# Three decoding passes for float64 weights instead of four, and a new set of ranks, in a downsampled-plus-local attention and gated MLP kernel

## The chip, the cores and the metric

One core of a Trainium2 chip runs the whole program. The metric is device microseconds of one launch. Three runs of the kernel before gave 586.04, 587.34 and 1143.34 us, median 587.34 us.

## The reference

For 8 batches and 8 heads of 576 positions by 64 dimensions, two attentions are added. The first averages q, k and v over groups of 4 positions, takes softmax attention over the 144 groups and repeats each result 4 times. The second is attention within a band: position i sees j only where |i - j| < 4.

```
pos = np.arange(S)
mask = np.abs(pos[:, None] - pos[None, :]) < factor
...
return (out_up + out_local).astype(np.float32)
```

The sum, with heads side by side, is x of shape (8, 576, 512). A gated MLP follows:

```
h = np.maximum(x @ w_in, 0.0)
u, v = (h[..., :d_ff // 2], h[..., d_ff // 2:])
v_n = (v - mu) / np.sqrt(var + 1e-06)
v_s = np.einsum('ts,bsd->btd', w_spatial, v_n) + b_spatial[None, :, None]
return ((u * v_s) @ w_out).astype(np.float32)
```

w_in (512 x 1024) and w_out (512 x 512) arrive as float64, which no engine of the kernel computes in: their 32-bit halves are read as integers and made into float32 on the chip.

## The kernel before

The work is a list of pieces. A piece is one instruction or a short group on one engine, with the buffers that it reads and writes, a planned duration and a rank. `Plan.run` walks the pieces as a list scheduler does: on each engine it takes, of the pieces that can start within NEAR ns of the first one that can, the one of lowest rank. What it emits is a fixed order for each engine; each engine then runs its instructions strictly in that order and waits at each for what it needs. The ranks stand in tables (RANK for attention, MRANK for the MLP, WRANK for the weights) and the strings in ON say, for the n-th piece of a kind, which engine or which variant it takes (A ScalarE, D VectorE, P GpSimd; for "mask", T adds the mask by a matmul and D on VectorE).

Names, used below as in the profile:

- Attention works on 32 pairs of heads (n = 0 to 31, four to a batch). S is the banded score matmul (L751 lays the mask down, L758 the scores), T transposes the probabilities (L854), AV multiplies by v (L962). Sd, Td, AVd are the same for the averaged attention (L820, L901, L929). With "sub" on A the maximum only becomes a bias (L790) and ScalarE does ten activations of 64 columns (L798); on D VectorE subtracts (two instructions, L786) and ScalarE does one activation of 640 columns (L801). "sum" (L730, L733) averages q and k; "normd" (L883 on ScalarE, L886 elsewhere) scales the averaged attention's probabilities. The result x of a pair is written as a high half on ScalarE (xa to xg, L1012) and a low half on VectorE (L1014), and its last 64 positions are copied to xtail (L1016).
- MLP, per batch: V are five matmul pieces (four of L1039, one tail L1044), evicted by L1057; U are eight (L1102, evicted by L1105); SP are eight (L1134, gated on L1155), O four (L1170) and one tail piece for two batches (L1185).
- Weights: w_in's V half (WV), its U half (WU), w_spatial (WSP) and w_out (WO). WV, WU and WO come in four pieces of 128 x 512 float64 each. A piece is fetched (L523) into stg or more, decoded into one of six buffers mba to mbf, summed up in absolute value on ScalarE (L658) for a scale, and split into a float16 high half on ScalarE (L511) and a low half on VectorE (L514). V of a batch needs all of WV and x of the batch's four pairs; U needs all of WU; SP all of WSP.
- The four decoding passes, per piece, are d1 (multiply the upper word, read as float32, by 2^-112; ScalarE L541, or VectorE or GpSimd L543), d2 (shift left by 3 and clear the sign, VectorE L546), d3 (fetch the sign from the product and join it, VectorE L550) and d4 (join the top three bits of the lower word, VectorE L555). GpSimd and VectorE pieces that the program holds to share a port carry `port=True` and are never planned at the same time; d4 does not carry it.
- Where the plan sees TensorE idle in the first 110 us it puts in filler matmuls on constants (L1214) that compute nothing.

In the order that results, the first 80 us hold the loads, the decoding and the attention of the first pairs, and the rest is the steady part in which the MLP of one batch is interleaved with the attention of the next.

Of the kernel before, what the change touches and what calls it, by code (L numbers as in the profile page):

```python
# [8 lines left out]
F32 = mybir.dt.float32  # L9
# [3 lines left out]
I32 = mybir.dt.int32  # L13
# [63 lines left out]
class Plan:  # L77
# [61 lines left out]
    def run(self, near=150.0, stay=0.0, dma=(1900.0, 900.0), emit=True):  # L139
# [17 lines left out]
        while left:  # L157
# [95 lines left out]
RANK = {"load": [90.169, 257.539, 303.907, -159.662, -510.639, -25.642, 405.455, -297.525, 5.13, 264.367, 351.699, 276.06,  # L253
            682.221, 54.868],
        "vload": [434.68, 234.812, 262.794, 74.315, 728.463, -15.228, -243.297, -31.858],
        "vabs": [467.345, -1170.291, -136.803, -260.041, -345.091, 133.278, -941.516, 12.316],
        "tv": [-84.809, 64.704, 479.328, 995.501, 350.344, -198.277, -346.695, -222.775],
        "sum": [-132.552, -211.417, -218.297, -329.655, 364.902, 111.471, 91.479, 393.607, 1763.478, 137.899, -76.822, 739.926,
            -40.013, 64.573],
        "S": [-671.111, -532.057, 271.346, -585.398, -841.898, 478.333, 18.826, -602.428, 177.33, 40.497, 208.693, 271.364,  # L260
            160.961, 247.816],
        "E": [-754.564, -306.398, -710.714, 213.708, 122.695, 238.643, 42.123, 1057.27, -571.18, -741.81, -241.921, -309.788,
            -379.446, -245.978],
        "N": [351.195, -536.694, -589.965, 590.836, -96.063, 629.51, 1122.526, -174.004, 0.365, -36.852, -359.038, -336.375,
            646.961, -94.987],
        "T": [-226.254, -238.971, -1086.855, -450.305, 760.115, -1472.718, -853.117, 276.295, 490.91, -182.776, -192.183,
            -37.547, -339.778, 39.198],
        "Sd": [85.837, -47.061, -984.686, -195.937, -159.211, -44.271, -280.964, 516.618, 1316.646, -337.627, -261.865, 184.375,
            -269.138, -135.441],
        "Nd": [271.663, -564.046, -555.506, -129.335, -1202.018, -327.324, -477.611, -101.539, -269.892, 119.203, 541.338, 147.5,  # L270
            341.705, 491.194],
        "Td": [-63.802, 166.781, 912.991, 171.397, -207.967, -74.563, 1024.918, -842.706, -306.265, 29.991, -143.29, -121.336,
            -992.41, -238.063],
        "AVd": [239.818, -835.613, -260.738, 73.129, 507.866, 908.357, 67.434, -40.584, -197.477, 92.972, -337.272, -1.96,
            -132.091, 143.162],
        "AV": [190.318, -438.664, -462.749, 692.051, -804.089, 72.948, 440.132, -392.904, -551.022, 39.946, -326.512, -51.248,
            5.793, -319.964],
        "X": [134.737, -356.693, 84.463, -85.637, -382.379, 453.739, 25.853, 353.509, 251.441, 230.484, -271.172, 149.233,
            -52.957, -25.463]}
MRANK = {"V": [[16.513, 67.783], [-623.639, -792.169], [-416.323, 106.304], [-263.565, -49.834], [-261.378, 39.119], [-352.403,  # L280
            38.031], [-368.389, 30.748], [-34.568, -55.986]],
        "U0": [[-275.497, 276.444], [50.68, -65.887], [170.332, 454.518], [262.672, -77.469], [-62.913, 15.29], [51.586,
# [977 lines left out]
```

## Time and profile before

| | |
|---|---|
| median of three runs | 587.34 us |
| the profiled execution | 586.45 us |
| its span, first to last instruction | 584.7 us |
| around the span | 1.75 us |
| TensorE busy | 557.9 us (95%) |
| VectorE busy | 419.0 us (72%) |
| ScalarE busy | 375.7 us (64%) |
| GpSimd busy | 181.5 us (31%) |
| mean granted TensorE clock | 0.988 |
| filler matmuls (L1214) | 89, of which one group of 88 is busy for 26.9 us |

A share of busy time is a mean over a first part in which TensorE has little to do and a long second part in which it has no pause; the two are to be read apart. The fillers count as busy TensorE time. A duration in a timeline row is that of one instruction; two instructions of one engine overlap a little, so that from start to start less time passes.

### The profile page before, as it was taken

How to read it: one execution, taken by the hardware profiler on the slowest of the kernel's cores; microseconds unless marked ns; L12 is line 12 of the kernel's file. 1: busy time of each engine (PE TensorE's matmuls, PEld its weight loads, DVE VectorE, ACT ScalarE, POOL GpSimd, SP SyncE). 2: the span in 40 equal slices, each digit the busy share in tenths (PEclk: the TensorE clock that was granted, in tenths of full speed). 3: DMA queues.
4: the chain of work that ended last, by engine and by line, in shares of the span. 5: the costliest groups of instructions: out<-in, count | busy, mean ns of one | idle time of the engine just before them, and what ended most of it. 6: DMA issues, size and time to landing. Idle time of an engine off the chain costs nothing.

```text
span 584.7 us, 16107 instructions
## 1 busy us (share of the span) xinstructions
PE 557.9 (95%) x6507; PEld 371.5 (64%) x6507; DVE 419.0 (72%) x1106; ACT 375.7 (64%) x1099; POOL 181.5 (31%) x203
## 2 busy tenths in 40 slices
PE   6678799999999999999999999999999999999997
PEld 2445356765677756766678855665678548865763
DVE  6888998997569769757797835997838775661640
ACT  4698897857578758747885544766765647653432
POOL 3525114202441283602541213513423346100200
PEclk9798899999999999999999999999999999999999
DMA  8986850224323327105332430524521410010002
GB/s 281 355 239 173 238 110 1 66 66 137 92 69 120 113 43 221 45 19 167 50 95 64 107 77 36 164 72 132 115 56 39 137 37 1 2 38 1 19 19 90
DMA packets 37390, 57.04 MB, mean 98 GB/s; under 512 B 3650, under 2 KB 24130, under 8 KB 37316
## 3 DMA queue, kind: packets, MB, share of 16 engines
q1 hardware_dynamic: 35012, 48.94, 26.3%
q0 software_dynamic: 2304, 7.08, 7.2%
q8 instruction: 51, 0.84, 0.6%
q14 instruction: 23, 0.19, 0.1%
HBM read 46.57 MB, written 9.44 MB: 96 GB/s over the span
## 4 chain that ended last, share of the span: by engine, by line
PE 83%; ACT 5%; DVE 5%; DMA 3%; issue 2%; SPq 1%; ACTq 0%; DVEq 0%
PE pma L1134 5%; PE pmd L1102 4%; PE pmb L1102 4%; PE pmc L1134 4%; PE pmb L1170 4%; PE pmd L1170 4%; PE pmc L1102 4%; PE pmd L1134 4%; PE pma L1170 4%; PE pma L1102 4%; PE pma L1039 4%; PE pmb L1134 3%; PE pmd L1039 3%; PE pmc L1170 3%; PE pmb L1039 3%; PE pmc L1039 3%
## 5 line engine op out<-in xcount | busy, mean ns | idle before, releaser
L1102 PEld LDWEIGHTS <-win 128*128 128x128 f16 x768 | 74.6, 98 | 20.4 <-issue 0.8
L1134 PEld LDWEIGHTS <-vha 128*128 128x128 f16 x768 | 73.9, 98 | 18.9 <-issue 0.4
L1170 PEld LDWEIGHTS <-gb 128*128 128x128 f16 x288 | 27.7, 98 | 31.3 <-issue 0.4
L1134 PE MATMUL pma<-wsp,vha 128*128 128x256 f16 (+1 forms) x240 | 32.1, 283 | 0.0
L1214 PE MATMUL pma<-mask_b,mask_a 128*128 128x512 bf16 x88 | 26.9, 446 | 3.1 <-DVE mask_a L384 3.1
L1134 PE MATMUL pmc<-wsp,vha 128*128 128x256 f16 (+1 forms) x204 | 27.6, 285 | 0.0
L1067 POOL TENSOR_TENSOR sta<-sta,mhalf 128x1 f32<-128x1 f32 (+1 forms) x12 | 8.6, 718 | 48.2 <-DVE sta L1051 44.3
L1134 PE MATMUL pmd<-wsp,vha 128*128 128x320 f16 (+1 forms) x168 | 22.9, 286 | 0.0
L1134 PE MATMUL pmb<-wsp,vha 128*128 128x320 f16 (+1 forms) x156 | 22.1, 291 | 0.0
L1170 PE MATMUL pmd<-wo,gb 128*128 128x512 f16 x96 | 22.0, 379 | 0.0
L730 POOL TENSOR_TENSOR sumb<-qkb 128x576 f32<-128x576 f32 x9 | 11.0, 1224 | 30.3 <-DMA qkb<-qk_dram 30.3
L1214 PEld LDWEIGHTS <-mask_a 128*128 128x128 bf16 x89 | 8.9, 110 | 16.5 <-issue 8.3
L1067 POOL TENSOR_TENSOR stc<-stc,mhalf 128x1 f32<-128x1 f32 (+1 forms) x15 | 10.2, 683 | 28.4 <-DVE stc L1051 28.4
L679 POOL DMA_DIRECT2D tva<-v_dram x12 | 10.8, 900 | 24.2 <-DMA tva<-v_dram 16.8
L1170 PE MATMUL pmb<-wo,gb 128*128 128x512 f16 x72 | 16.5, 379 | 0.0
L1039 PEld LDWEIGHTS <-xa 128*128 128x128 f16 x96 | 9.4, 98 | 11.1 <-issue 0.5
L1170 PEld LDWEIGHTS <-ga 128*128 128x128 f16 x96 | 9.1, 98 | 10.1 <-issue 0.4
L1170 PE MATMUL pma<-wo,gb 128*128 128x512 f16 x60 | 13.8, 379 | 0.0
L1170 PE MATMUL pmc<-wo,gb 128*128 128x512 f16 x60 | 13.8, 379 | 0.0
L1067 POOL TENSOR_TENSOR stb<-stb,mhalf 128x1 f32<-128x1 f32 (+1 forms) x13 | 9.1, 698 | 13.0 <-DVE stb L1051 6.1
L872 POOL TENSOR_SCALAR smdc<-smdc 112x3 f32<-112x3 f32 x2 | 0.4, 198 | 38.6 <-ACT eda L868 28.9
L679 POOL DMA_DIRECT2D tvb<-v_dram x12 | 10.8, 902 | 4.6 <-DMA tvb<-v_dram 4.3
(1119 smaller groups left out, 1724.4 us busy)
## 6 DMA issues: line engine op xcount, KB each, us to landing
qka<-qk_dram SPq DMA_DIRECT2D x15, 576.0 KB
qkb<-qk_dram SPq DMA_DIRECT2D x15, 576.0 KB, 4.6
tva<-v_dram POOLq DMA_DIRECT2D x12, 288.0 KB, 5.2
tvb<-v_dram POOLq DMA_DIRECT2D x12, 288.0 KB, 4.4
stg<-w_in_dram SPq DMA_DIRECT2D x5, 512.0 KB, 10.6
out_dram<-rowb SPq DMA_DIRECT2D x8, 256.0 KB, 3.7
out_dram<-rowc SPq DMA_DIRECT2D x7, 256.0 KB, 2.0
out_dram<-rowa SPq DMA_DIRECT2D x7, 256.0 KB, 2.4
```

What stands on the lines that cost most here:

```text
L679: plan.op("POOL", 850, lambda r=r: nc.gpsimd.dma_start(t.ap[LOW:KEYS], v4[b, r], accum_op=ALU.add), w=[t], rank=rank + 2.0 + 0.3 * r, kb=2 ...
L730: side(s1).tensor_tensor(sb.ap.rearrange("p x (g r) -> p x g r", r=2), x[:, :, :, :2], x[:, :, :, 2:], op=ALU.add)
L872: side(ivd).tensor_scalar(smd.ap[:PD], smd.ap[:PD], 1.0e-9, 4.0, op0=ALU.add, op1=ALU.mult)
L1039: nc.tensor.matmul(ps.ap, xs[c].ap[:, i, t * P:(t + 1) * P], win[:, c, j, FF:], start=(c == 0 and (i, j) == (0, 0)), stop=(c == NC - 1 and ...
L1067: plan.op("POOL", 530, lambda: nc.gpsimd.tensor_tensor(st.ap[:r, 8:9], st.ap[:r, 8:9], mhalf[:r], op=ALU.pow), w=[st], rank=rank - EVICT, ...
L1102: nc.tensor.matmul(ps.ap[:, :n], win[:, c, i, ft * P:(ft + 1) * P], xs[c].ap[:, j, HA[h]:HA[h + 1]], start=(c == 0 and (i, j) == (0, 0)), ...
L1134: nc.tensor.matmul(ps.ap[:, :n], vh.ap[:, c, i, fs], wsp[:, c, j, hs], start=(c == 0 and (i, j) == (0, 0)), stop=False)
L1170: nc.tensor.matmul(ps.ap, g.ap[:, c, HA[1] * i + k:HA[1] * i + k + P], wo[:, c, j, :], start=(c == 0 and (i, j) == (0, 0)), stop=(c == NF ...
L1214: nc.tensor.matmul(ap.rearrange("p (j k) -> p j k", k=64), mask_a, mask_b[:, None, :].broadcast_to([P, 8, 64]), start=True, stop=True)
```

## The change

The first pass becomes a parametric Relu on ScalarE for all twelve pieces: a negative input is multiplied by 2^-112 and by -2^32, which makes it positive and puts 32 on its exponent, so that the sign stands as one exponent bit. The shift by 3 moves this bit into the sign's place, no mask is needed, and d3 is gone. What was d4 is now d3 and carries `port=True`. The tables RANK, MRANK and WRANK, the numbers EVICT, NEAR and STAY and the strings of ON are new throughout.

```
-RANK = {"load": [90.169, 257.539, 303.907, -159.662, ...
+RANK = {"load": [143.005, 47.751, 252.982, -69.47, ...
...
-ON = {"sub": "AAAAADDAAAAAADADDAADADDDDAADDDDA",
+ON = {"sub": "DDDDDDADDADAAADDDADDAAADDDA",
...
-        "sum": "DPPDDPDPDDDPPPDDDPPDPDDPDDDDPPDP",
-        "d1": "AAAPADDDADDP",
-        "mask": "TTTTTTTTDDDDDTD",
-        "norm": "PDPDPDPDDPPDPPDPDDDPDDPPDPPPD",
-        "normd": "AAAPADAAPADDAPPDADAPPDDAPPDAADPA",
+        "sum": "DPPPDPPPDDPDPPDDDDPPDPDDDDPDDDPD",
+        "mask": "TTTTTTTTD",
+        "norm": "PDPPPDPDPPDDDPDPPPDPDPDPPPPDDPD",
+        "normd": "PAAPPDPPAAADDPAAPAPADAAPPPPADDAP",
...
         def d1():
             lo, hi = words()
-            if w1.eng == "ACT":
-                nc.scalar.mul(eb.ap, hi.bitcast(F32), 2.0**-112)
-            else:
-                side(w1).tensor_scalar(eb.ap, hi.bitcast(F32), 2.0**-112, None, op0=ALU.mult)
+            nc.scalar.activation(eb.ap, hi.bitcast(F32), AF.Prelu, scale=2.0**-112, alpha=-2.0**32)
         def d2():
-            nc.vector.tensor_scalar(mb.ap.bitcast(I32), eb.ap.bitcast(I32), 3, 0x7FFFFFF8, op0=ALU.logical_shift_left, op1=ALU.bitwise_and)
+            nc.vector.tensor_scalar(mb.ap.bitcast(I32), eb.ap.bitcast(I32), 3, None, op0=ALU.logical_shift_left)
         def d3():
-            m = mb.ap.bitcast(I32)
-            nc.vector.scalar_tensor_tensor(m, eb.ap.bitcast(I32), -2**31, m, op0=ALU.bitwise_and, op1=ALU.bitwise_or)
-
-        def d4():
             lo, hi = words()
             m = mb.ap.bitcast(I32)
             nc.vector.scalar_tensor_tensor(m, lo, 29, m, op0=ALU.logical_shift_right, op1=ALU.bitwise_or)
-        w1 = Way("d1", i, A=("ACT", 590, False), P=("POOL", 1530, True), D=("DVE", 335, True))
-        plan.op(w1, 0, d1, r=[t], w=[eb], hold=[mb], rank=rank, name="d1")
+        plan.op("ACT", 590, d1, r=[t], w=[eb], hold=[mb], rank=rank, name="d1")
         plan.op("DVE", 335, d2, r=[eb], w=[mb], rank=rank, port=True, name="d2")
-        plan.op("DVE", 602, d3, r=[eb], w=[mb], rank=rank, port=True, name="d3")
-        plan.op("DVE", 602, d4, r=[t], w=[mb], rank=rank, name="d4")
+        plan.op("DVE", 602, d3, r=[t], w=[mb], rank=rank, port=True, name="d3")
```

Most line numbers after the edit are smaller by 10 (L1057 becomes L1047, L511 becomes L510, L514 becomes L513, L541 becomes L539).

On VectorE, the first decoded weights and the first pairs of heads, as they stood before (mba and mbb are decoded weights, rowa and rowb the results of d1, suma and kda the averages of a pair, mxa its maximum):

```order
10 L546 TENSOR_SCALAR mba<-rowa 128x512
11 L550 SCALAR_TENSOR_TENSOR mba<-rowa,mba 128x512
12 L555 SCALAR_TENSOR_TENSOR mba<-stg,mba 128x512
13 L546 TENSOR_SCALAR mbb<-rowb 128x512
14 L550 SCALAR_TENSOR_TENSOR mbb<-rowb,mbb 128x512
15 L730 TENSOR_TENSOR suma<-qka 128x576
16 L555 SCALAR_TENSOR_TENSOR mbb<-stg,mbb 128x512
17 L733 TENSOR_TENSOR kda<-suma 128x288
18 L780 TENSOR_REDUCE mxa<-paa 128x10
```

And the same place after the change:

```order
10 L542 TENSOR_SCALAR mba<-rowa 128x512
11 L547 SCALAR_TENSOR_TENSOR mba<-stg,mba 128x512
12 L542 TENSOR_SCALAR mbb<-rowb 128x512
13 L547 SCALAR_TENSOR_TENSOR mbb<-stg,mbb 128x512
14 L720 TENSOR_TENSOR suma<-qka 128x576
15 L723 TENSOR_TENSOR kda<-suma 128x288
16 L770 TENSOR_REDUCE mxa<-paa 128x10
17 L776 TENSOR_TENSOR sa<-paa,mxa 128x2x3x64
18 L776 TENSOR_TENSOR sa<-paa,mxa 128x2x2x64
```

A decoded piece takes two instructions instead of three, and the first pair's maximum is now subtracted on VectorE (L776), so that ScalarE needs one activation for that pair in place of ten.

On ScalarE, from the last x of the first batch (xd, high half) on, before; win are the split weights of w_in, here those of U from mbc to mbf, rowe is the first evicted V piece, vg and va are v tiles of the next batch:

```order
99 L1012 ACTIVATE xd<-xfa,sxa 128x576
100 L511 ACTIVATE win<-mbf,sw 128x512
101 L511 ACTIVATE win<-mbe,sw 128x512
102 L511 ACTIVATE win<-mbd,sw 128x512
103 L696 ACTIVATE junk,sxb<-vg 128x640
104 L1016 COPY xtaila<-xd 128x128
105 L511 ACTIVATE win<-mbc,sw 128x512
106 L933 COPY dnb<-pab 128x144
107 L904 COPY pdTa<-pma 100x288
108 L696 ACTIVATE junk,sxb<-va 128x640
109 L1057 ACTIVATE rowe<-pmb,sx2a 128x512
```

After the change xd's high half is row 93, and fourteen rows later this follows:

```order
107 L1047 ACTIVATE rowd<-pmb,sx2a 128x512
108 L686 ACTIVATE junk,sxb<-va 128x640
109 L510 ACTIVATE win<-mbf,sw 128x512
110 L510 ACTIVATE win<-mbc,sw 128x512
111 L1047 ACTIVATE rowa<-pma,sx2a 128x512
112 L510 ACTIVATE win<-mbd,sw 128x512
113 L539 ACTIVATE rowe<-stg 128x512
114 L686 ACTIVATE junk,sxa<-vb 128x640
115 L1047 ACTIVATE rowc<-pmd,sx2a 128x512
116 L510 ACTIVATE win<-mbe,sw 128x512
```

The splits of U's weights stood ahead of the first evicted V piece; now they stand between the V pieces, the last of them behind the third. TensorE follows this: before it ran two V pieces ahead of the first U, now it runs four. The splits of w_spatial, which stood ahead of xd, now stand behind it.

## Rows read from the trace of the kernel before

**Rows 1.** Busy time of each engine by stretch, us, and granted clock, DMA share, GB/s.

```profile
core 0: us, PE busy (x) PEld busy (x) DVE busy (x) ACT busy (x) POOL busy (x), PEclk, DMA share, GB/s
0.00:20.00 20.00, 14.37 (x171) 6.63 (x171) 14.73 (x26) 7.74 (x24) 9.99 (x24) 1.00 0.90 315
20.00:40.00 20.00, 13.27 (x173) 8.44 (x173) 17.27 (x47) 18.22 (x74) 6.21 (x7) 0.83 0.95 268
40.00:60.00 20.00, 16.18 (x280) 10.39 (x281) 17.96 (x52) 17.88 (x53) 7.70 (x8) 0.91 0.72 206
60.00:80.00 20.00, 15.53 (x190) 8.57 (x190) 18.93 (x55) 17.77 (x44) 2.49 (x3) 0.91 0.85 215
80.00:550.00 470.00, 467.96 (x5508) 319.15 (x5506) 341.31 (x906) 304.90 (x888) 155.13 (x162) 1.00 0.27 75
550.00:585.00 35.00, 30.61 (x191) 18.34 (x189) 8.78 (x26) 9.21 (x20) 0.00 (x0) 1.00 0.16 53
```

**Rows 2.** Timeline from 78 to 86 us: start us, us, engine, line, instruction.

```profile
78.18 0.78 ACT L1012 ACTIVATE xd<-xfa,sxa 128x576 f16<-128x576 f32 x1
79.30 0.76 DVE L1014 SCALAR_TENSOR_TENSOR xd<-xfa,sxa,xd 128x576 f16<-128x576 f32 x1
...
80.05 0.81 PE L1039 MATMUL pmb<-win,xa 128*128 128x512 f16 x3
...
81.78 0.72 ACT L511 ACTIVATE win<-mbc,sw 128x512 f16<-128x512 f32 x1
...
82.86 0.74 DVE L514 SCALAR_TENSOR_TENSOR win<-mbc,sw,win 128x512 f16<-128x512 f32 x1
...
85.70 0.49 PE L1102 MATMUL pmc<-xa,win 128*128 128x256 f16 x3
```

**Rows 3.** Timeline, instructions of the decoding (d1 on VectorE and ScalarE, d3).

```profile
56.27 0.41 DVE L543 TENSOR_SCALAR rowb<-more 128x512 f32<-128x512 f32 x1
...
57.53 0.70 ACT L541 ACTIVATE rowa<-stg 128x512 f32<-128x512 f32 x1
...
60.47 0.68 DVE L550 SCALAR_TENSOR_TENSOR mbc<-rowc,mbc 128x512 int32<-128x512 int32 x1
...
61.07 0.69 DVE L550 SCALAR_TENSOR_TENSOR mbb<-rowa,mbb 128x512 int32<-128x512 int32 x1
```

**Rows 4.** L798 in the first 80 us: stretch, ScalarE busy (instructions), clock, DMA, GB/s.

```profile
0.00:80.00 80.00, 10.69 (x50) 0.91 0.86 251
```

**Rows 5.** L801, the one-activation form: duration ns min/median/max.

```profile
L801 ACT ACTIVATE sa<-sa x6: 730/736/743, 59.2 to 492.7; 128x640 f32<-128x640 f32 x6
```

**Rows 6.** Timeline: a pair's scores, subtraction, scaling of the averaged attention, average.

```profile
45.87 0.81 PE L758 MATMUL pab<-qkb 64*64 64x64 f32 x40
...
48.21 0.89 DVE L786 TENSOR_TENSOR sc<-pab,mxb 128x384 f32<-128x384 f32 x2
...
49.08 1.03 ACT L883 ACTIVATE eda<-eda,smda 112x144 f32<-112x144 f32 x3 [0.90 <-POOL smda L874]
...
50.50 0.84 DVE L730 TENSOR_TENSOR suma<-qka 128x576 f32<-128x576 f32 x1
```

**Rows 7.** Timeline from 16 to 20 us: a decoding pass on VectorE, averages on GpSimd.

```profile
16.03 4.67 DVE L555 SCALAR_TENSOR_TENSOR mbc<-more,mbc 128x512 int32<-128x512 int32 x1
16.35 1.46 POOL L730 TENSOR_TENSOR sumb<-qkb 128x576 f32<-128x576 f32 x1
...
19.19 0.95 POOL L733 TENSOR_TENSOR kdc<-suma 128x288 f32<-128x288 f32 x1
```

**Rows 8.** The only activation table load, duration ns.

```profile
L541 ACT ACT_TABLE_LOAD  x1: 1283/1283/1283, 0.7 to 0.7; - x1
```

**Rows 9.** Chain that ended last, one V piece: start us, us.

```profile
95.54 2.59 PE pma L1039 x12
```

**Rows 10.** Timeline, the tail's half-height copy and the last output transfer's issue.

```profile
576.24 0.68 ACT L1191 ACTIVATE rowe<-pmb,aub 64x512 f32<-64x512 f32 x1
...
581.41 0.34 SPq L1175 DMA_DIRECT2D out_dram<-rowc  x1
```

More of the change, by code (lines that the diff above doesn't have):

```diff
@@ L247, in run @@
         return end
[L253 to L279, printed above, removed]
@@ new lines @@
+MRANK = {"V": [[-120.813, 103.137], [-373.166, -785.223], [-588.287, 86.439], [-457.053, -295.554], [-271.069, 53.075],
+            [-161.929, 7.172], [-384.75, 67.584], [1.753, -86.54]],
+        "U0": [[-381.018, 507.475], [-225.844, -398.15], [392.079, 353.99], [415.277, -261.891], [-69.09, -16.703], [-362.251,
+            -497.795], [59.314, -190.411], [573.297, -308.684]],
+        "S0": [[631.14, 127.639], [-206.013, -184.383], [299.174, 561.899], [-372.357, 30.262], [381.875, 239.103], [33.324,
+            19.169], [-136.587, -125.569], [104.744, -531.737]],
+        "U1": [[66.951, 205.966], [432.921, 80.243], [202.58, -320.842], [-584.875, -261.385], [85.111, -539.421], [-290.079,
+            -515.53], [-73.151, -407.568], [-105.893, -362.577]],
+        "O0": [[170.632, -34.982], [-172.469, 696.573], [159.95, -390.053], [-841.668, -359.026], [22.932, -667.87], [-349.956,
+            231.605], [321.827, -73.48], [-54.093, -578.395]],
+        "S1": [[-122.247, -1002.997], [272.521, 179.124], [-502.627, -34.942], [83.425, -28.324], [193.115, 251.294], [212.725,
+            -514.576], [-0.655, 14.458], [254.101, -410.908]],
+        "O1": [[-425.021, 297.386], [239.962, 469.652], [56.568, -208.235], [-194.872, 129.628], [-641.125, -6.104], [281.584,
+            274.929], [184.644, 89.516], [19.298, 376.248]]}
@@ new lines @@
+EVICT = 456.633
+WRANK = {"WV load": [31.22, -21.921, 242.309, 4.474],
+        "WV decode": [350.543, -287.444, -567.367, 661.466],
+        "WV bound": [-83.736, 162.235, 909.503, 36.755, -835.361],
+        "WV split": [-201.598, 11.031, -341.826, -1007.43],
+        "WU load": [-364.293, 427.826, 390.089, -59.831],
+        "WU decode": [387.574, -316.232, 1019.795, 459.568],
+        "WU bound": [1425.684, -228.293, 245.85, 118.051, 725.352],
+        "WU split": [-187.848, -607.313, -258.771, -328.661],
+        "WSP load": [289.708, -579.107, 622.627, -316.354, 744.76],
+        "WSP bound": [397.382, 106.669, -930.598, 200.751, 873.332, -382.338],
+        "WSP split": [-150.625, -91.686, 309.424, 430.824, -1165.74],
+        "WO load": [201.774, -325.888, 429.457, 987.307],
+        "WO decode": [137.835, 619.019, -225.889, -8.083],
+        "WO bound": [-64.148, 457.463, -289.1, 18.247, -58.582],
+        "WO split": [620.04, -563.746, 894.059, 1022.164]}
@@ L313 @@
+NEAR = 104.496
+STAY = 26.882
 WARM = 110000.0
```

65 lines of the change are left out of this document (30 added, 35 removed).

## The prediction

> **What bounds the kernel now.** First read the busy time by stretch [rows 1]. From 80 to 550 us TensorE pauses for 470 − 467.96 = 2.0 us, at a granted clock of 1.00: that part is TensorE's own work, which the change does not touch (the matmul pieces are the same but for one mask). In the first 80 us TensorE's busy share is no measure, since 89 fillers are in it. There, from 20 us on, VectorE is busy 54.2 and ScalarE 53.9 of 60 us, and the transfers hold 0.72 to 0.95 of the DMA engines. In the first 20 us ScalarE is busy for 7.74 only: it waits for loads. So the time is the start of continuous matmul work, plus a fixed 500 us, plus a tail.
>
> Second, the timeline where that work starts [rows 2]. The high half of xd, the last of the first batch's x, ends on ScalarE at 78.96, the low half on VectorE at 80.06, and V's first matmul starts at 80.05 (its trio for xd comes last). U's last split ends at 82.50 on ScalarE and 83.60 on VectorE, and U starts at 85.70, when two V pieces of 2.59 us each [rows 9] are through. What the change gains must come from these two points: how early V starts, and how early U's weights are there.
>
> **The change part by part.** I count, on each engine's order, all rows up to xd, and multiply by durations.
>
> VectorE (row 172 before, 146 after):
> - the old d3: nine of the twelve stood ahead of xd. Start to start of two in a row is 61.07 − 60.47 = 0.60 us [rows 3]: −5.4.
> - d1: three stood here, 0.41 each [rows 3], now on ScalarE: −1.2.
> - w_spatial's four low halves and three smaller pieces of it move behind xd, at the 0.74 of a split [rows 2]: −5.2. This is moved, not saved.
> - two pairs' averages go to GpSimd, 0.84 [rows 6] and a second step about half as long: −2.5.
> - four more pairs subtract on VectorE, 0.89 each [rows 6]: +3.6.
> - the rest (one decoded piece more, some small ones fewer) I put at nothing.
> Sum: −10.7 us.
>
> ScalarE (row 99 before, 93 after):
> - ten activations cost a pair 10.69 / 5 = 2.14 [rows 4], the single one 0.74 [rows 5]. Five pairs took the first form, now one does: −4 × 2.14 + 4 × 0.74 = −5.6.
> - five more d1 at 0.70 [rows 3]: +3.5. The parametric form I price as the plain multiply. No row shows it; it is one activation of the same 512 columns, so between the 0.70 of this row and twice that, 3.5 more; I take 0.70.
> - three pairs' scaling of the averaged attention, 1.03 each [rows 6], goes to GpSimd: −3.1.
> - w_spatial's four high halves and three tail pieces move behind xd, at 0.72 [rows 2]: −5.0.
> Sum: −10.2 us.
>
> The row of d1 says 0.70 on ScalarE against 0.41 on VectorE. The Trainium skill (ScalarE: Activation LUTs, Rules for kernel authors) says to do relu and multiplications on VectorE. The rows agree for one instruction, and by the rule alone five moved passes would make the change dearer by 5 × 0.29 = 1.5 us; but here a pass of 0.60 goes for each, and the sum goes by the engine counts above.
>
> If both engines waited exactly as long as before, V would start some 10 us earlier. I do not take all of it. Of the roughly 10.5 us, three old d3 and one pair's ten activations (1.8 + 1.4, and a d1 or average) stand in the first 20 us, where loads set the pace [rows 1]: about 4 us of it turns into waiting. The ends are 0 (the loads, at 0.95 of the DMA engines from 20 to 40 us, give the pace of the whole head) and 10.5; I take 6.3. V then starts at 80.05 − 6.3 = 73.8, and xd's high half ends on ScalarE at 78.96 − 6.3 = 72.7.
>
> Now U. Before, six ScalarE rows lay between xd and U's last split; now twenty-three do: six splits and three tail pieces at 0.72, three evictions of V and a d1 at about 0.70, four sums over v tiles, a pair's exponentials and copies, about 13.8 us together by my count. So U's last high half ends at 72.7 + 13.8 = 86.5 and, with the low half and the hops of before (83.60 − 82.50 = 1.1), U starts at 87.6, against 85.70: 1.9 later. V's four pieces end at 73.8 + 4 × 2.59 = 84.2 and a few tenths, so TensorE stands for about 3 us before U. That is the new wait of this order, and ScalarE sets it.
>
> But by then TensorE has done more. Two V pieces more: 2 × 2.59 = 5.2. Of the attention, scores, transpose and values of one pair more, and of the averaged attention two pieces fewer; each is near the 0.81 of the scores [rows 6], with the mask somewhat more: +1.3. Gain at U's start: 6.5 − 1.9 = 4.6 us.
>
> Behind U, the w_spatial splits that were moved must be done before SP. U's eight pieces, V's fifth and some attention keep TensorE for about 15 us, and ScalarE needs about as long for its rows up to U's last eviction; I cost it at nothing, and if that cover fails by a microsecond, so does the gain.
>
> Smaller terms. One pair fewer lays its mask by matmul: −0.3. The new order ends with the tail piece of two half-height copies, one after the other, instead of one full copy: +0.7, the 0.68 of the second copy [rows 10]; the last output's issue at 581.41 and what follows stay. GpSimd gets about 10 us more in all; it was busy 155 of 470, and TensorE does not wait for it; nothing, but see the rivals.
>
> Sum, against the profiled execution's 586.45 (span 584.7 and 1.75 around it): −4.6 − 0.3 + 0.7 = −4.2, so 582.2 us. The median of the runs, 587.34, is 0.9 above that execution; I leave this inside the range.
>
> **The rivals.**
> *All of it, and the blocked pass too.* One decoding pass of 0.69 took 4.67 us at 16.03 and ended at 20.70, just after GpSimd's averages ended at 20.14 [rows 7]: 4.0 us of VectorE lost. The pass now carries the port mark, so the plan keeps the two apart. The Trainium skill (SBUF — State Buffer, SBUF: two separate sides) says that a VectorE instruction with two SBUF inputs and a GpSimd one that reads SBUF lock each other out for a whole instruction; by that rule the row's block is a lock that the new order avoids. If the 4.0 us and the full 10.5 both reach U, the time is 582.2 − 4.2 − 4.0 = 574.0. For it: both engines were 90% busy. Against it: the block lies at 16 us, where loads rule, and the new order still carries 85 fillers in place of 89, so its plan expects TensorE to idle about as long.
>
> *The loads set the head.* xd stays at 80, ScalarE's 13.8 us follow, U starts at 78.96 + 13.8 + 1.1 = 93.9, 8.2 later, against 6.5 us of extra work done: 586.45 + 1.7 + 0.4 = 588.6. For it: 0.86 of the DMA engines over 80 us. Against: the loads that V needs end with the first batch's last v tile, and VectorE, not the transfers, was busy 18.93 of the last 20 us.
>
> *Blocks in the steady part (slower).* GpSimd has more to do there, and an eviction on VectorE that it blocks for 4.0 us [rows 7] stops TensorE once its four PSUM banks are full. If that happens once a batch for seven batches and half of it is covered, 582.2 + 7 × 2.0 = 596.2. It decides from 4.2 us of new pauses between 80 and 550 us. For it: every place in the order is new. Against: 2.0 us of pauses now, with VectorE at 73% in this part.
>
> *Table loads.* If the parametric form needed another table than Exp, each of twelve would cost two loads of 1.283 [rows 8], up to 31 us: 613. The order lists a single load, as before, so this is next to excluded.
>
> **How the numbers follow.** Forecast 0.60, the full gain 0.10, the loads 0.17, the blocks 0.12, table loads 0.01. A difference of 2% is 11.7 us and about what a measurement of this kernel tells from none. Faster by more than that takes the full gain (0.07 of its 0.10, and 0.02 from the forecast's edge): 0.09. Slower by more takes pauses above 16 us (0.04) or the tables: 0.05. Within 2%: 0.86. The range goes from 575, short of the full gain, to 591, past the loads and into the milder blocks.
>
> **What would show it.** Right: one table load; d1 near 0.70 us, twelve times on ScalarE; V's first matmul near 74 and U's near 87.6, with a pause of some 3 us between four V pieces and U that ends with U's last split; TensorE pauses of about 2 us from there to 550; the last copy 0.7 later after the last matmul. Wrong: V near 80 (the loads), V before 71 with no pause at U (the full gain), more than 5 us of pauses after 90 us (the blocks), or d1 above 1 us.

## The result and the profile after

The changed kernel took 580.22 us (median of four runs, 579.15 to 580.97) against 587.34 for the kernel before in the same set (median of three runs): the ratio on record is 0.9882, 95% interval 0.9852 to 0.9911. A fourth run of the kernel before, of 1143.34 us, fell in a slow state and is left aside. A second set gave 579.90 against 587.31, and 0.9871 (0.9849 to 0.9893). So it is faster by 1.2%, which is less than 2%. The profiled execution took 580.97, the slowest of the ten, with a span of 579.1; the one of before took 586.45 with 584.7. What follows explains these 5.5 us first, and then what is left to the medians' 7.1 and 7.4.

Busy time by stretch (us, PE busy, PEld, DVE, ACT, POOL, granted clock, DMA share, GB/s), which answers to [rows 1]:

```profile
core 0: us, PE busy (x) PEld busy (x) DVE busy (x) ACT busy (x) POOL busy (x), PEclk, DMA share, GB/s
0.00:20.00 20.00, 12.64 (x152) 6.06 (x156) 13.14 (x28) 8.43 (x19) 9.14 (x24) 0.91 0.91 312
20.00:40.00 20.00, 15.69 (x197) 9.10 (x186) 17.09 (x45) 13.36 (x41) 8.59 (x10) 1.00 0.92 246
40.00:60.00 20.00, 15.55 (x319) 9.88 (x316) 19.38 (x48) 19.41 (x54) 10.76 (x11) 1.00 0.82 256
60.00:80.00 20.00, 17.87 (x260) 10.44 (x259) 18.29 (x55) 19.12 (x55) 10.52 (x12) 1.00 0.87 214
80.00:550.00 470.00, 465.75 (x5463) 319.76 (x5462) 341.71 (x899) 308.30 (x894) 147.67 (x158) 1.00 0.26 74
550.00:579.00 29.00, 24.11 (x133) 12.74 (x131) 4.45 (x12) 7.71 (x16) 0.00 (x0) 0.95 0.19 64
```

From 20 to 550 us TensorE's granted clock is 1.00 in every stretch; before it was 0.83, 0.91 and 0.91 between 20 and 80 us. VectorE and ScalarE are nearly full only from 40 us on. From 80 to 550 us TensorE's pauses grew from 2.0 to 470 − 465.75 = 4.25 us.

The timeline where the continuous matmul work starts (start us, us, engine, line, instruction, idle time before it and what ended it), which answers to [rows 2]:

```profile
67.98 0.82 ACT L1002 ACTIVATE xd<-xfa,sxa 128x576 f16<-128x576 f32 x1
...
68.80 0.73 DVE L636 TENSOR_REDUCE sw<-pab 128x1 f32<-128x576 f32 x1
...
68.96 0.69 ACT L846 COPY probTa<-paa 128x640 f32<-128x640 f32 x1
...
69.71 0.91 PE L952 MATMUL paa<-probTa,ve 64*64 64x60 f32 x40
...
70.73 0.71 DVE L971 TENSOR_TENSOR xfb<-paa,dna 128x232 f32<-128x232 f32 x2 [0.57 <-PE paa L952]
...
71.54 0.81 DVE L1004 SCALAR_TENSOR_TENSOR xd<-xfa,sxa,xd 128x576 f16<-128x576 f32 x1
...
72.42 0.82 PE L1029 MATMUL pmb<-win,xa 128*128 128x512 f16 x3
...
82.07 0.74 ACT L510 ACTIVATE win<-mbe,sw 128x512 f16<-128x512 f32 x1
...
83.23 0.74 DVE L513 SCALAR_TENSOR_TENSOR win<-mbe,sw,win 128x512 f16<-128x512 f32 x1
83.48 0.38 PE L1092 MATMUL pma<-xa,win 128*128 128x256 f16 x2
...
84.03 0.28 PE L1092 MATMUL pma<-xa,win 128*128 128x256 f16 x1 [0.17 <-DVE win L513]
```

The high half of xd ends at 68.80, which is 10.2 us earlier than before, the low half at 72.35 (7.7 earlier), V starts at 72.42 (7.6 earlier) and U at 83.48 (2.2 earlier) with a pause of 0.17. Before, the low half ended 1.1 us behind the high half; now it ends 3.55 behind. The rows between say why. From the end of the high half to the start of the low half (68.80 to 71.54) VectorE spends 1.36 us on small rows for w_spatial's scale (L636 and four behind it, up to 70.16), waits for 0.57, and spends 0.81 on the scaling of a pair's attention (L971, L973). The wait is for TensorE (L952), which waits for ScalarE's copy of that pair's probabilities (L846), and that copy stands behind xd's high half with one short copy between.

The first rows of the decoding's activation by line (duration ns min/median/max, first and last start us), which answer to [rows 3, 8], and one pass of the timeline, which answers to [rows 7]:

```profile
L539 ACT ACTIVATE rowa<-stg x4: 663/692/770, 5.8 to 89.8; 128x512 f32<-128x512 f32 x4
L539 ACT ACTIVATE rowe<-stg x2: 667/672/676, 24.7 to 80.2; 128x512 f32<-128x512 f32 x2
L539 ACT ACT_TABLE_LOAD  x1: 1283/1283/1283, 0.7 to 0.7; - x1
```

```profile
17.88 0.68 DVE L547 SCALAR_TENSOR_TENSOR mbc<-more,mbc 128x512 int32<-128x512 int32 x1
```

The parametric form costs what the plain multiply did, 0.66 to 0.79 us over all twelve, and there is one table load. The pass that took 4.67 us at 16 us now takes 0.68.

The largest new pause of TensorE behind U, from the timeline, with what VectorE did before it:

```profile
103.94 0.73 DVE L513 SCALAR_TENSOR_TENSOR wo<-mbf,sw,wo 128x512 f16<-128x512 f32 x1
104.59 0.73 DVE L513 SCALAR_TENSOR_TENSOR wo<-mbc,sw,wo 128x512 f16<-128x512 f32 x1
...
105.25 0.80 DVE L1004 SCALAR_TENSOR_TENSOR xf<-xfa,sxb,xf 128x576 f16<-128x576 f32 x1
105.98 0.14 DVE L1105 TENSOR_SCALAR aua<-pmd 128x1 f32<-128x1 f32 x1
...
106.17 1.11 PE L1124 MATMUL pmd<-wsp,vha 128*128 128x320 f16 x7 [1.34 <-DVE aua L1105]
```

TensorE waits 1.34 us there to write a PSUM tile (pmd) that VectorE reads with a tiny instruction (L1105), and that instruction is queued behind two splits of the output weights and one of x.

The tail, which answers to [rows 10]; TensorE's last matmul ends at 574.11:

```profile
571.36 2.75 PE L1175 MATMUL pmd<-wo,gta 128*128 128x512 f16 x12
...
574.20 0.68 ACT L1181 ACTIVATE rowc<-pmd,aua 64x512 f32<-64x512 f32 x1 [1.90 <-PE pmd L1175]
...
574.91 0.68 ACT L1181 ACTIVATE rowc<-pmd,aub 64x512 f32<-64x512 f32 x1
```

The two half-height copies now stand last. From the last matmul to the end of the span it is 4.96 us; before it was 584.65 − 580.61 = 4.04.

The sum of the profiled executions. U starts 85.70 − 83.48 = 2.2 us earlier; from U's start to the last matmul it was 494.91 and is 490.63, 4.3 less, in which pauses grew by 2.35 (1.85 before, 4.20 now), so that 6.6 us of TensorE's work had been done earlier; the tail is 0.9 longer. −2.2 − 4.3 + 0.9 = −5.6, the difference of the spans. The second profiled execution of the changed kernel (579.21, span 577.3) had about the same pauses (4.4) and started V at 70.51 and U at 81.57: the 1.8 us by which it was shorter lie ahead of V. The medians' difference is larger than that of the profiles from both sides: this execution was 0.8 slower than its kernel's median, and the one of before 0.9 faster than its own.

### The profile page after: what moved, and what is told of

It reads as the page before. It is cut to its first block, busy times and chain, and to the rows that moved or that the text cites. A ratio compares the mean times of both kernels' runs of the same rounds, so it can differ in the third digit from the quotient of the medians.

```text
span 579.1 us, 16048 instructions
## 1 busy us (share of the span) xinstructions
PE 551.6 (95%) x6501; PEld 368.0 (64%) x6501; DVE 414.1 (72%) x1084; ACT 376.3 (65%) x1076; POOL 186.7 (32%) x213
## 4 chain that ended last, share of the span: by engine, by line
PE 70%; DVE 18%; ACT 6%; issue 2%; DMA 2%; POOL 0%; SPq 0%; ACTq 0%; DVEq 0%; POOLq 0%
PE pmd L1124 4%; PE pma L1124 4%; PE pmb L1160 4%; PE pma L1160 4%; PE pmc L1029 4%; PE pmc L1160 4%; PE pma L1029 4%; PE pmc L1124 3%; PE pmb L1124 3%; PE pmd L1029 3%; PE pmd L1092 2%; PE pma L1092 2%; PE pmc L1092 2%; PE pmb L1029 2%; PE pmd L1160 2%
## 5 line engine op out<-in xcount | busy, mean ns | idle before, releaser
L1124 PE MATMUL pma<-wsp,vha 128*128 128x256 f16 (+1 forms) x216 | 29.4, 286 | 0.0
L1124 PE MATMUL pmd<-wsp,vha 128*128 128x256 f16 (+1 forms) x204 | 27.6, 285 | 1.3 <-DVE aua L1105 1.3
L1204 PE MATMUL pma<-mask_b,mask_a 128*128 128x512 bf16 x83 | 23.4, 415 | 3.1 <-DVE mask_a L383 3.1
L1124 PE MATMUL pmb<-wsp,vha 128*128 128x256 f16 (+1 forms) x180 | 24.1, 283 | 0.0
L1124 PE MATMUL pmc<-wsp,vha 128*128 128x320 f16 (+1 forms) x168 | 23.5, 290 | 0.0
L1160 PE MATMUL pmb<-wo,gb 128*128 128x512 f16 x96 | 22.0, 379 | 0.0
L1057 POOL TENSOR_TENSOR sta<-sta,mhalf 128x1 f32<-128x1 f32 (+1 forms) x14 | 9.0, 646 | 32.3 <-DVE sta L1041 32.3
L1160 PE MATMUL pma<-wo,gb 128*128 128x512 f16 x72 | 16.5, 379 | 0.0
L720 POOL TENSOR_TENSOR suma<-qka 128x576 f32<-128x576 f32 x6 | 7.8, 1294 | 23.4 <-DMA qka<-qk_dram 23.4
L1057 POOL TENSOR_TENSOR stb<-stb,mhalf 128x1 f32<-128x1 f32 (+1 forms) x15 | 10.9, 725 | 11.4 <-DVE stb L1041 11.4
L1160 PE MATMUL pmc<-wo,gb 128*128 128x512 f16 x60 | 13.8, 379 | 0.0
L1057 POOL TENSOR_TENSOR stc<-stc,mhalf 128x1 f32<-128x1 f32 (+1 forms) x11 | 7.5, 678 | 18.7 <-DVE stc L1041 15.2
L720 POOL TENSOR_TENSOR sumb<-qkb 128x576 f32<-128x576 f32 x6 | 7.8, 1296 | 16.5 <-DMA qkb<-qk_dram 16.5
```

Source lines behind the costliest of these rows:

```text
L720: side(s1).tensor_tensor(sb.ap.rearrange("p x (g r) -> p x g r", r=2), x[:, :, :, :2], x[:, :, :, 2:], op=ALU.add)
L1057: plan.op("POOL", 530, lambda: nc.gpsimd.tensor_tensor(st.ap[:r, 8:9], st.ap[:r, 8:9], mhalf[:r], op=ALU.pow), w=[st], rank=rank - EVICT, ...
L1124: nc.tensor.matmul(ps.ap[:, :n], vh.ap[:, c, i, fs], wsp[:, c, j, hs], start=(c == 0 and (i, j) == (0, 0)), stop=False)
L1160: nc.tensor.matmul(ps.ap, g.ap[:, c, HA[1] * i + k:HA[1] * i + k + P], wo[:, c, j, :], start=(c == 0 and (i, j) == (0, 0)), stop=(c == NF ...
L1204: nc.tensor.matmul(ap.rearrange("p (j k) -> p j k", k=64), mask_a, mask_b[:, None, :].broadcast_to([P, 8, 64]), start=True, stop=True)
```

## The experiments

Seven kernels keep the order of the changed kernel or of before, instruction by instruction, and give back or take away work. Four give the planner something else, and the changed kernel was run once more. Medians stand beside the kernel before on the same chip in each set: 587.46, 586.92 and 587.31.

**The removed pass given back, in the new order.**

```diff
         def d2():
             nc.vector.tensor_scalar(mb.ap.bitcast(I32), eb.ap.bitcast(I32), 3, None, op0=ALU.logical_shift_left)
+            m = mb.ap.bitcast(I32)
+            nc.vector.scalar_tensor_tensor(m, eb.ap.bitcast(I32), -2**31, m, op0=ALU.bitwise_and, op1=ALU.bitwise_or)
```

> The changed kernel, in its own fixed order, with the removed VectorE pass given back to all twelve pieces (it writes the sign bit once more, so nothing else changes). Ten of the twelve stand ahead of the first batch's last x, at 0.60 us each, three of them in the first 20 us; one more stands between it and U. VectorE theory (VectorE's work ahead of the last x sets V, and VectorE then sets U): seven passes after the first 20 us give 4.2 us and the eleventh up to 0.6, with the three early ones lost in waits for loads: V's first matmul at 76.6 to 78.5, and 584.5 to 585.0 us against 580.2 for the changed kernel; 586.8 if nothing is lost. Order theory (the passes are small beside what the new order and picks earn): under 1.5 us, 581.7 at most. Loads theory (the transfers pace the head): no change, 580.2.

588.64 us, ratio to before 1.0018 (1.0000 to 1.0036): 8.4 us above the changed kernel, more than any of the theories allowed, for twelve passes that cost 12 × 0.60 = 7.2 us if nothing hides them. V started at 78.76 and U at 89.82, both 6.3 later than in the changed kernel's profile, and the pauses from 80 to 550 us grew to 470 − 463.89 = 6.1. So the new order and picks gain nothing with the old amount of decoding: with it they are as slow as before. That takes the order theory and the loads theory out. Why it costs more than its passes is in two views of this kernel, the timeline at 58 us and the stretches that follow:

```profile
58.46 2.38 DVE L544 SCALAR_TENSOR_TENSOR mbd<-rowb,mbd 128x512 int32<-128x512 int32 x1
60.77 1.15 DVE L549 SCALAR_TENSOR_TENSOR mbb<-more,mbb 128x512 int32<-128x512 int32 x1
```

```profile
60.00:65.00 5.00, 1.26 (x15) 0.56 (x13) 4.93 (x9) 2.91 (x7) 1.30 (x2) 0.74 1.01 319
65.00:70.00 5.00, 5.00 (x59) 2.17 (x52) 3.95 (x14) 4.72 (x18) 1.32 (x3) 0.58 1.04 220
```

One given-back pass took 2.38 us beside GpSimd's work (the two steps of an average run there from 59.16 to 61.37). That is 1.7 us above the usual 0.69, and it belongs to this experiment and not to the pass: the planner, which keeps marked pieces off GpSimd's, did not know of it. TensorE was left with 1.26 us of work in the 5 us from 60 on, and its granted clock fell, to 0.58 in the next 5 us, most of it at the lower of its two levels, where the changed kernel has 1.00.

**The same for the first three pieces alone.**

```diff
+            m = mb.ap.bitcast(I32)
+            if key[0] == "WV" and key[1] < 3:
+                nc.vector.scalar_tensor_tensor(m, eb.ap.bitcast(I32), -2**31, m, op0=ALU.bitwise_and, op1=ALU.bitwise_or)
```

> The same, for the three pieces alone that are decoded in the first 20 us. If what is saved there turns into waits for loads, as the prediction has it, nothing changes: the last x within 0.3 us of the changed kernel's 68.80 (high half) and 580.2 us. If it reaches V, it is 3 x 0.60 = 1.8 us: 582.0.

581.07 us (579.22 to 582.61), ratio 0.9899 (0.9874 to 0.9923), which is 0.9 to 1.2 above the changed kernel; xd's high half ended at 69.17 and its low half at 73.37, 0.4 and 1.0 later. It lies between the two expectations. V differs by 1.9 us between two executions of the changed kernel itself, and the granted clock here was 0.71 from 65 to 70 us, where the changed kernel has 1.00; so this run does not show whether the early passes reach V.

**ScalarE's activation twice, in the new order.**

```diff
             lo, hi = words()
+            nc.scalar.activation(junk[:, :FF], hi.bitcast(F32), AF.Prelu, scale=2.0**-112, alpha=-2.0**32)
             nc.scalar.activation(eb.ap, hi.bitcast(F32), AF.Prelu, scale=2.0**-112, alpha=-2.0**32)
```

> The changed kernel, in its own fixed order, with every piece's parametric activation done twice on ScalarE (the first one into scratch): ten times some 0.70 us ahead of the last x, three of them in the first 20 us, and one more before U. Prediction's theory (ScalarE sets the last x and U): 4.9 us and 0.7 for U, so 585 to 586 us. VectorE theory: at the last x ScalarE runs some 2.7 us ahead (high half done at 68.80, low half begun at 71.54), and that is eaten first: 2.2 us, some 582.5, and U is then set by ScalarE with a pause of about 1 us. Loads theory: 580.2.

584.15 us, ratio 0.9951 (0.9932 to 0.9970): 3.9 above the changed kernel for some 12 × 0.7 = 8.4 us of work, where VectorE's 7.2 cost 8.4, or some 6.7 if the blocked pass's 1.7 is set apart (an estimate, as if all of it had reached the end). That lies between the theories. In the profiles xd's high half, its low half and U all moved by 1.7. So per microsecond of work VectorE weighs about twice as much as ScalarE. But the picture of a ScalarE that runs ahead, whose lead is eaten first, does not fit: the two halves of xd moved together, and VectorE waited for the chain L846, L952, L971 ahead of the low half as long as in the changed kernel (0.57).

**The pass taken away, in the order of before** (this kernel leaves the weights' sign out).

```diff
         def d3():
-            m = mb.ap.bitcast(I32)
-            nc.vector.scalar_tensor_tensor(m, eb.ap.bitcast(I32), -2**31, m, op0=ALU.bitwise_and, op1=ALU.bitwise_or)
+            return
```

> The kernel before, in its own fixed order, without the third decoding pass: the sign of the float64 weights is left out, all else is done. Nine passes of 0.60 us stood ahead of the last x, three of them in the first 20 us. VectorE theory: 3.6 us for the six later ones, 583.7 us (581.9 if nothing is lost), V near 76.5 against 80.05. Prediction's theory that ScalarE too is full: between 584 and 586.5, since ScalarE's rows do not move. Order or loads theory: 586.5 to 587.5.

586.39 us, ratio 0.9975 (0.9955 to 0.9995): 1.1 us. The same pass that is worth 8.4 in the new order is worth 1.1 in the old one. Its timeline, and its stretches from 65 to 80 us (columns as above):

```profile
77.61 0.76 DVE L1013 SCALAR_TENSOR_TENSOR xd<-xfa,sxa,xd 128x576 f16<-128x576 f32 x1
...
79.79 1.01 PE L1038 MATMUL pmb<-win,xa 128*128 128x512 f16 x3
```

```profile
65.00:70.00 5.00, 2.75 (x14) 1.13 (x13) 3.99 (x14) 4.61 (x15) 0.83 (x1) 1.00 1.10 236
70.00:75.00 5.00, 3.26 (x103) 2.52 (x103) 4.93 (x11) 4.80 (x11) 0.83 (x1) 1.00 0.88 193
75.00:80.00 5.00, 4.19 (x41) 3.28 (x40) 4.86 (x16) 4.77 (x13) 0.83 (x1) 0.68 0.72 143
```

Only 1.7 of the nine passes' 5.4 us reached xd (its low half ended at 78.37, before at 80.06), and of these V got 0.26. xd's high half moved by the same 1.7, which fits ScalarE's rows as what held the rest, but no run shows that by itself. V started 1.4 us behind xd, while TensorE finished attention work queued ahead of it at a granted clock of 0.68: it had been busy for only 2.75 and 3.26 us of the two stretches before. The kernel before has its 0.66 at 70 to 75 us, and 1.00 from 75 to 80.

**Tables and decode crossed.** Old ranks and picks with the new decode, new ones with the old decode, and before with nothing but the mark on its fourth pass:

```diff
-        plan.op("DVE", 602, d4, r=[t], w=[mb], rank=rank, name="d4")
+        plan.op("DVE", 602, d4, r=[t], w=[mb], rank=rank, port=True, name="d4")
```

> The kernel before with its own tables of ranks and picks, but the three-pass decode of the change; the planner makes an order of its own from them. VectorE theory (the pass is worth several us wherever it goes): 581 to 584 us, V before 77. Theory that both are needed (given an order made for four passes, the pass alone gave 1.07 us of 587.46): 585 to 588, V at 79 or later, or pauses behind U that take the rest. Port theory (the mark on the last pass avoids the 4.0 us of a blocked pass): no decoding pass above 1.5 us, and 4 us less than 587.5.

> The changed kernel's tables of ranks and picks with the four-pass decode of before (the multiply on ScalarE, the third pass on VectorE); the planner makes an order of its own from them. Order theory (the new order and picks earn the gain by themselves): 580 to 582 us. Theory that both are needed: 586.5 to 589, as the fixed order with the pass given back (588.64).

> The kernel before with the port mark on its fourth pass and nothing else changed; the planner makes a new order with it. Port theory: the pass at 16 us takes 0.7 in place of 4.67 us, and 2 to 4 us are gained: 583.5 to 585.5. Loads theory for the first 20 us (what is saved there turns into waits): 586.5 to 588.5.

629.07, 626.68 and 637.98 us: ratios 1.0704 (1.0678 to 1.0731), 1.0659 (1.0631 to 1.0688) and 1.0860 (1.0833 to 1.0886), 40 to 51 us slower than before, far from every expectation. Busy time from 80 to 550 us, in this sequence:

```profile
80.00:550.00 470.00, 449.93 (x5359) 306.46 (x5360) 324.85 (x853) 290.13 (x847) 144.08 (x154) 0.98 0.27 75
```

```profile
80.00:550.00 470.00, 439.82 (x5246) 298.75 (x5245) 325.62 (x867) 294.12 (x862) 144.54 (x151) 0.97 0.28 75
```

```profile
80.00:550.00 470.00, 444.82 (x5184) 301.45 (x5175) 326.18 (x864) 287.05 (x833) 151.42 (x155) 0.97 0.28 73
```

TensorE pauses for 20 to 30 us where before it paused for 2.0. A table of ranks belongs to one list of instructions with one set of costs and marks: a single mark changes the planner's choices from there on, and all the later ranks then steer a program that they were not made for. So these three say nothing on the decode or the port mark, and only kernels with an order held fixed can.

**ScalarE alone, and both engines, relieved in the order of before.** Five pairs' ten exponentials become one; then the pass is left out as well (attention of five pairs, and the weights' sign, are not the reference's).

```diff
             t = ps.ap.rearrange("p (h j k) -> p h j k", h=2, k=64)
+            if n < 5:
+                src = t[:, :, :NBLK] if pe_mask else s.ap.rearrange("p (h j) k -> p h j k", h=2)
+                nc.scalar.activation(s.ap.rearrange("p (h j) k -> p h j k", h=2), src, AF.Exp, bias=mx.ap[:, :1], scale=1.0 / 8.0)
+                return
             for j in range(NBLK):
```

> The kernel before, in its own fixed order, with one exponential over the whole tile in place of ten for the first five pairs that use ten (nine of the ten blocks get the first one's bias, so the attention of these pairs is not the reference's): ScalarE alone is relieved, by 5 x 1.4 = 7.0 us ahead of V. Theory of two engines that hold each other (the order of before waits on both, and one alone gains little): 585 to 587 us, V at 78.5 or later. ScalarE theory: 581 to 583, V near 74. TensorE's own rows ahead of V as the limit: V not before 79.5 and 587.

> Both reliefs in the order of before: ten exponentials made one for five pairs, and the third decoding pass left out (the sign of the float64 weights and the attention of five pairs are not the reference's). Theory of two engines that hold each other: more than the two alone together, 580 to 583 us, V at 74 to 76. Theory that the order of before is held by something else (its transfers, or TensorE's own rows): V not before 78 and 585 to 587.

ScalarE alone: 585.31 us, 0.9958 (0.9933 to 0.9983), 2.0 less. Both: 579.87, 0.9893 (0.9859 to 0.9927), 7.4 less, where the single reliefs add up to 3.1. These medians fit two engines that hold each other. By the ratios it is 6.3 (4.3 to 8.3) for both, against 2.5 (1.0 to 3.9) for ScalarE and 1.5 (0.3 to 2.6) for the pass, so the surplus is not clear of noise. Nor do the profiles show it. The second kernel's six runs go from 579.67 to 585.61, and its profile is of the slowest. The kernel before, then ScalarE alone, then both, with the stretches in the same sequence:

```profile
78.29 0.48 PE L820 MATMUL paa<-kdb 64*64 64x144 f32 x8 [0.85 <-DVE xfa L983]
```

```profile
74.22 0.76 PE L824 MATMUL paa<-kdb 64*64 64x144 f32 x8 [0.84 <-DVE xfa L987]
...
75.23 0.76 DVE L1018 SCALAR_TENSOR_TENSOR xd<-xfa,sxa,xd 128x576 f16<-128x576 f32 x1
...
77.50 1.49 PE L1043 MATMUL pmb<-win,xa 128*128 128x512 f16 x3
...
81.37 0.81 PE L1043 MATMUL pma<-win,xa 128*128 128x512 f16 x3
```

```profile
75.02 0.76 DVE L1017 SCALAR_TENSOR_TENSOR xd<-xfa,sxa,xd 128x576 f16<-128x576 f32 x1
...
77.30 1.49 PE L1042 MATMUL pmb<-win,xa 128*128 128x512 f16 x3
...
81.46 0.81 PE L1042 MATMUL pma<-win,xa 128*128 128x512 f16 x3
```

```profile
75.00:80.00 5.00, 5.00 (x32) 3.00 (x28) 4.93 (x13) 4.62 (x11) 0.00 (x0) 0.50 0.49 86
```

```profile
70.00:75.00 5.00, 3.05 (x42) 2.30 (x44) 4.83 (x19) 4.58 (x13) 0.83 (x1) 0.87 0.80 190
75.00:80.00 5.00, 5.00 (x32) 2.93 (x25) 4.97 (x12) 4.41 (x11) 0.00 (x0) 0.50 0.42 63
```

With ScalarE alone relieved xd was there at 75.99, 4.1 us earlier than before and with all of VectorE's rows in place; without the pass as well it was there at 75.78. V, at 77.50 and 77.30, lies between the expectations of both theories. So in these two executions VectorE did not hold xd back, against the theory of two engines that hold each other. They do not decide it either, since the second is that kernel's slowest, with a clock of 0.57 from 25 to 30 us where the first had 1.00. What took the gain is seen behind xd. In both, TensorE ran at a granted clock of 0.50, the 1.2 GHz level, from 75 to 80 us, where the kernel before had 1.00. From the first of the attention matmuls queued right ahead of V (L820 before) to V it was 80.05 − 78.29 = 1.76 us before, and 3.28 and 3.29 here, so that V started 1.5 us behind xd. V's first three matmuls took 1.49 in place of 0.81, and its first piece 3.87 and 4.16 from start to start in place of 2.59 [rows 9]. Together that is 2.8 and 3.1 us of the gain lost at the lower clock.

Over the six runs of the kernel with both reliefs the mean granted clock and the time go together: 0.997 to 0.999 gave 579.67 to 579.96 four times, 0.994 gave 582.82, 0.987 gave 585.61. With ScalarE alone it is the same: 582.69 and 582.70 at 0.996, 587.43 at 0.987. Compared at like clocks, leaving out the pass as well is worth some 1 to 3 us, an estimate from these runs.

**No block at 16 us, in the order of before** (the averaged attention of two pairs is left out).

```diff
         def sum1():
+            if b == 0 and s1.eng == "POOL":
+                return
...
         def sum2():
+            if b == 0 and s1.eng == "POOL":
+                nc.gpsimd.memset(kb.ap, 0.001)
+                return
```

> The kernel before, in its own fixed order, with GpSimd's averages of the two pairs at 16 to 20 us left out (a constant is written in their place, so the averaged attention of these pairs is not the reference's), so that nothing on GpSimd stands beside the decoding pass that took 4.67 us. If that block lies where loads set the pace (the prediction): 586.5 to 588 us. If its 4.0 us reach V: 583 to 584.

584.84 us, 0.9953 (0.9935 to 0.9971): 2.5 less. With nothing reading on GpSimd beside it, the pass took its usual time:

```profile
16.00 0.68 DVE L555 SCALAR_TENSOR_TENSOR mbc<-more,mbc 128x512 int32<-128x512 int32 x1
```

That is 4.0 us less, and xd's low half ended at 76.90, 3.2 earlier: in this order what is lost at 16 us is not swallowed by waits for loads. (GpSimd was free 2.9 us earlier too, at 17.23 in place of 20.14, which this run does not tell apart.) V again came 1.5 us behind xd, with the clock at 0.66 from 75 to 80 us. ScalarE had also waited for the blocked pass, as its first row behind it in the kernel before shows:

```profile
20.79 0.63 ACT L658 ACTIVATE junk<-mbc 128x512 bf16<-128x512 f32 x1 [4.45 <-DVE mbc L555]
```

**The tail piece ahead of the last full piece, in the changed kernel.**

```diff
-            rank = R["O1"](2)
+            rank = R["O1"](0.5 if b == B - 1 else 2)
```

> The changed kernel with the last batch's tail piece of the output ranked ahead of its last full piece; the planner makes a new order with it. If the two half-height copies at the end are what makes the stretch behind the last matmul 0.92 us longer (4.96 against 4.04), that stretch comes back to 4.0 to 4.2 us, and the time is 579.3 (0.7 to 0.9 less) as long as the rest of the order keeps; if the stretch keeps near 5, the cause was something else.

578.12 us (577.91 to 578.91), ratio 0.9843 (0.9821 to 0.9866). The planner's order differs from that of the changed kernel only at the end, and there it does what was expected; TensorE's last matmul ends at 572.81 of 576.85, so the tail is 4.04 us:

```profile
570.31 0.68 ACT L1181 ACTIVATE rowe<-pmb,aua 64x512 f32<-64x512 f32 x1 [1.90 <-PE pmb L1175]
571.02 0.68 ACT L1181 ACTIVATE rowe<-pmb,aub 64x512 f32<-64x512 f32 x1
...
572.90 0.69 ACT L1164 ACTIVATE rowc<-pmd,aub 128x512 f32<-128x512 f32 x1 [1.20 <-issue]
```

**The changed kernel once more.**

> The changed kernel itself, once more, timed in the same rounds as the others: 579 to 581 us. It tells whether the 578.12 of the kernel with the tail piece ranked ahead is more than the 0.9 us of its tail.

579.90 us (579.10 to 580.47), 0.9871 (0.9849 to 0.9893). The kernel with the moved tail lies 1.8 below it, in another set; 0.9 of that is its tail, by its trace, and the rest is not explained, and the two intervals overlap. Its median is the lowest seen here.

## Why the prediction was right, and where it was not

The forecast was 582.2 in 575 to 591 and within 2%; the profiled execution took 580.97 and the medians are 580.22 and 579.90. The verdict and the range held, and so did several terms. Two steps were wrong, in opposite directions, so that a time within 1.2 us of the forecast owes something to luck.

- **The single costs held.** The parametric activation at 0.70 us (0.66 to 0.79 measured, one table load); ScalarE's work ahead of xd, 10.2 us less by the count, and xd's high half did end 10.2 earlier (12.1 in the second execution, so that the agreement to a tenth is chance); the 13.8 us from xd's high half to U's last split (82.81 − 68.80 = 14.0); the work that TensorE has done by U, 6.5 and 0.3 for the mask (6.6); the tail, 0.7 (0.9, and the kernel with the moved tail gives it back).
- **The step that failed first: "about 4 us of it turns into waiting", and xd and V 6.3 earlier.** On ScalarE nothing was lost, so U's last split came 4 us earlier than forecast, U started at 83.48 in place of 87.6, and the pause of 3 us ahead of U was 0.17. The reason given, that loads swallow what is saved in the first 20 us, is contradicted, in the order of before, by the kernel without the block, where 3.2 of 4.0 us saved at 16 us reached xd. Part of ScalarE's idle time there, which the text put down to loads, was a wait for the blocked pass (4.45 us up to 20.79). For VectorE the forecast came out near (V at 72.42 against 73.8; 70.51 in the second execution), but what was lost went at the end, 2.4 us between the two halves of xd: rows for w_spatial's scale, a pair's scaling and a wait of 0.57 stand in VectorE's queue there.
- **The step that failed second: everything behind U "at nothing".** The text had said that if this cover fails by a microsecond, so does the gain. Pauses grew by 2.35 us: four of 0.7 to 1.3 stand there now. The largest, 1.34 at 106 us, is the cover's failure and is shown; it hangs on VectorE's queue, where splits of the output weights stand ahead of a short instruction, and not on ScalarE's, which the forecast had watched. The other three (0.71, 0.76 and 0.81, between 225 and 266 us) stand in the part that the text held to be untouched by the change; the profile puts two of them down to VectorE and one to ScalarE, and what moved them there was not tested.
- **By terms:** U 4.1 us earlier than forecast, pauses 2.35 and tail 0.2 longer, work 0.2 less: about 1.3 in all, as 580.97 stands to 582.2.
- **The rival of the full gain and the blocked pass** was half right in its mechanism. The second execution, with V at 70.51 and a pause of 0.17 us at U, even shows the sign that the text gave for it. But U at 81.57 stood 2.2 us behind that rival's 87.6 − 8.2 = 79.4, and the pauses and the tail had grown, so that this execution took 579.21 and not 574. The block was worth 2.5 us in the order of before. The Trainium skill (SBUF — State Buffer, SBUF: two separate sides) says that of a VectorE instruction with two SBUF inputs and a GpSimd one that reads SBUF, the one that starts first holds a shared pair of ports for its whole length and the other fully blocks. The traces agree that the two hold each other up: 4.67 us beside GpSimd's averages, 0.68 without them, 2.38 for a given-back pass at 58 us. They do not settle which one waits: by the recorded starts the pass at 16 us began at 16.03, behind a DMA issue of GpSimd at 15.72 but ahead of the first step of the averages at 16.35, and it ended behind the last of four. The change avoids it at 16 us; whether by the mark or by the new order is open, since the mark alone makes the planner build another program (637.98).
- **The rivals of loads and of table loads** fell: V came 7.6 earlier, and the table is loaded once. Blocks in the steady part fell too: the pauses total 4.2 us, 2.3 of them new, where that rival decided from 4.2 of new ones.

What the forecast did not have at all is that the parts depend on each other. The pass left out of the old order gains 1.1; the new order and picks with the pass given back lose 1.2 (588.64 against 587.46), some 1.7 of it to the blocked pass; together they gain 7.4. So neither the removed pass nor the new order is enough by itself. Why the pass gains so little in the old order is only in part shown. Its trace has 1.7 of 5.4 us at xd, with ScalarE's half of xd moved by no more. And in all four relieved kernels in that order TensorE, left short of work, then met V at a lower clock: the same rows ahead of V took 1.76 us before and 3.2 to 3.3 in these. That VectorE and ScalarE hold each other there is argued from the medians, 2.0 and 1.1 alone and 7.4 together; their intervals leave it open, and the profiles do not show it.

In the new order, from 40 to 550 us, the granted clock is 1.00 in both profiles of the changed kernel and in that of the moved tail. How much of the gain is the clock and how much the queues was not separated: no run here holds the clock fixed.

## What to carry to other kernels

What a removed instruction is worth depends on the order that it stood in: the same pass was worth 1.1 us in one order and 8.4, some 1.7 of it from a block, in another. So cost such a change as a whole, on every engine that its result passes through, and look at the next engine's state when it arrives: in the old order here TensorE had a lower clock when its inputs came earlier. A delay early in a long chain is not free because loads are slow there: look whether the engine that waits does wait for a load, or for the one that you relieve. And where a table of numbers steers a planner, compare versions with the order held fixed, by editing inside the instructions; a crossed table measures only that the table no longer fits.

## What the hardware showed that was not expected

Runs of one and the same program differ by several microseconds together with TensorE's mean granted clock, which falls in the head. Over the 58 runs of the kernel before that stand beside the experiments, the median was 589.4 us at a mean granted clock of 0.984 (nine runs) and 586.3 at 0.994 (twelve). In the traces the low stretches come behind stretches in which TensorE was partly idle (2.75 and 3.26 of 5 us, then 0.68; 1.26 of 5, then 0.58), though not every such stretch is followed by one: the changed kernel was busy for 3.22 of 5 us from 60 to 65 and kept 1.00. So a change that only empties TensorE's queue ahead of a critical matmul can lose at the matmul part of what it gained in front of it, 1.4 to 1.5 us ahead of V in four kernels here.

A pass with a single SBUF input was stretched beside GpSimd as well, in the changed kernel's timeline, from its usual 0.42 to 1.48 us, while GpSimd scaled a pair's probabilities from 49.77 to 51.56:

```profile
49.77 1.79 POOL L836 TENSOR_TENSOR sb<-sb,smb 128x640 f32<-128x640 f32 x1 [0.51 <-DVE smb L801]
...
50.36 1.48 DVE L542 TENSOR_SCALAR mba<-rowa 128x512 int32<-128x512 int32 x1
```
